# Moving the q and k transposes of four batches from TensorE to the transfer queue, with PV in quarters and in pairs

## The chip, the cores and the metric

One core of one Trainium2 chip runs the kernel. The metric is the device time of one execution in microseconds (us). Most comparisons use several rounds, in which the kernel and the kernel before ran in turn on the same chip. The start and length of each profiled execution are read from its trace.

In the profile PE is TensorE (matmul), DVE is VectorE, ACT is ScalarE, POOL is GpSimd, SP is SyncE, whose queue carries most transfers. "L754" is line 754 of that kernel's file. Lines shift between the kernels, so tile names are the safer label: b1p, op, osb, uT, qraw.

## The reference, cut to what matters

Eight batches of sparse attention (a window of 32 to each side, and eight global positions), whose result is the input of a token and channel MLP:

```python
batch, n_heads, seq, head_dim = (8, 8, 576, 64)
d_model, d_tok, d_ch = 512, 256, 1536
...
mask = (np.abs(pos[:, None] - pos[None, :]) <= 32) | is_global[:, None] | is_global[None, :]
attn = softmax(np.where(mask, scale * q @ k.T, -1e9))          # condensed
x = (attn @ v) as (batch, seq, heads * head_dim)               # condensed
h = np.maximum(xt @ w_tok1, 0.0) @ w_tok2                      # token MLP, over seq
u = x + h.transpose(0, 2, 1)
h2 = np.maximum(u @ w_ch1, 0.0) @ w_ch2                        # channel MLP
return (u + h2).astype(np.float32)
```

## The kernel before

The channel MLP of batch b is the dense part of a period: `M4` (first product, 12 groups of four matmuls into PSUM tile b1p, each evicted by ScalarE with the ReLU), then `M5` (second product, PSUM tile op, added to u by VectorE into an output buffer osb and stored). `first_half(b)` and `second_half(b)` weave attention of later batches between the dense groups. In their lists a `D` stands for one dense group; everything else is put between. The order of these lists is the order of instructions on every engine.

```python
def T(b, p):                                  # q and k of head pair p: 8 transposes on TensorE
    pT = (psm if b in (0, 2) else pss)([P, 2, 512], F16, name=f"pT_{b}_{p}")
    for ti, n in enumerate((qn, kn)):
        for i in range(4):
            nc.tensor.transpose(
                out=pT[:, ti, P * i : P * i + P], in_=n[b % 2][:, i, 2 * p : 2 * p + 2, :], identity=ident
            )
...
def TEq(b, p, eng=nc.vector.tensor_copy):     # VectorE empties PSUM, with a permutation of the columns
    eng(
        out=qTs[b % 2][:, p, 0:4, NG:QS].rearrange("p t (x i) -> p t x i", i=4),
        in_=st[b]["pT", p][:, 0].rearrange("p (i t x) -> p t x i", i=4, t=4),
    )
...
def M3(b, part):                              # u is transposed by the transfer queue for M4
    ...
            nc.sync.dma_start_transpose(out=s["uT"][:, :, P * tau : P * tau + P], in_=s["u16"][:, tau, :])
...
def M4(b, j):
    ps = psm([P, 512], name=f"b1p_{b}_{j}")   # psm: two buffers, shared with op
    for cc in range(4):
        nc.tensor.matmul(...)
    nc.scalar.activation(out=s["b1"][:, j, :], in_=ps, func=AF.Relu)
...
def M5(b, tau, part):
    ...                                       # op in psm; part 1 ends with:
        osb = ob.tile([P, DM], F32, tag="osb", name=f"osb_{b}_{tau}")
        nc.vector.tensor_add(out=osb, in0=s["u16"][:, tau], in1=ps)
        nc.sync.dma_start(out=out[b, P * tau : P * tau + P, :], in_=osb)
...
# in first_half(b), n = b + 1, m = b + 2; c(k) are two of ScalarE's casts of q and k of batch m
u = [D, D, pv(0), D, pv(1), *c(0), D, pv(2), *c(1), D, pv(3), lambda: [M1(n, ch) for ch in range(3)], *c(2), D]
u += [pv(4), *([lambda: TR(m)] if m < B else []), *tt(0), *c(3), D, lambda: M1(n, 3), D, lambda: M1(n, 4), *c(4)]
...
u += [lambda: (load_rest(m + 1), load_qk(m + 1, slice(0, H)))]        # only if m + 1 < B
u += [*tt(1), D, D, lambda: (M2(n, 0), M3(n, 0)), D, lambda: (M2(n, 1), M3(n, 1)), *tt(2), D]
```

The softmax here doesn't subtract the row's maximum and nothing guards it: scores larger than these inputs give would overflow.

Of the kernel before, what the change touches and what calls it, by code (L numbers as in the profile page):

```python
# [15 lines left out]
P = 128  # L16
NT = 5
NG = 8
# [26 lines left out]
def kernel(  # L45
# [342 lines left out]
    def casts(b):  # L388
        return [lambda ti=ti, p=p: cast_qk(b, ti, p, nc.scalar.copy) for p in (None, 0, 1, 2, 3) for ti in range(2)]
# [4 lines left out]
        )  # L394

    def T(b, p):
        pT = (psm if b in (0, 2) else pss)([P, 2, 512], F16, name=f"pT_{b}_{p}")
        for ti, n in enumerate((qn, kn)):
            for i in range(4):
                nc.tensor.transpose(  # L400
                    out=pT[:, ti, P * i : P * i + P], in_=n[b % 2][:, i, 2 * p : 2 * p + 2, :], identity=ident
                )
        st[b]["pT", p] = pT
# [13 lines left out]
    def TE(b, p):  # L417
        TEq(b, p)
        TEk(b, p)

    def TR(b):
        pr = (psm if b in (0, 2) else pss)([P, 2, 4, NP * 16], name=f"pr_{b}")
        sel = ident.rearrange("p (n r x) -> p r n x", n=NP, r=2)
        for ti, n in enumerate((qr, kr)):
            for i in range(4):
                for par in range(2):
                    nc.tensor.matmul(
                        pr[64 * par : 64 * par + 64, ti, i, :], lhsT=n[b % 2][:, i, :], rhs=sel[:, par], start=True, stop=True
                    )
        st[b]["pr"] = pr  # L430
        if b > 0:
            TRE(b)
# [214 lines left out]
    def PV(b, tau):  # L647
        s = st[b]

        sh = 64 if tau == NT - 1 and b % 2 == 1 else 0  # L650
        tiles = ((2 * tau, 0), (2 * tau + 1, 64)) if tau < NT - 1 else ((2 * tau, sh),)
        ps = (pss if b != 2 and tau % 2 else psv)([P, 2, 512], name=f"pv_{b}_{tau}")

        def glob(hf):
            for t, r0 in tiles:
                nc.tensor.matmul(  # L656
                    ps[r0 : r0 + 64, hf, 0 : NP * VW], lhsT=s["lf"][:, HQ * t : HQ * t + HQ],
                    rhs=s["rf"][:, 2 * hf : 2 * hf + 2], start=True, stop=False,
                )

        def local(hf, hh):
            h = NP * hf + hh
            for t, r0 in tiles:
                lo = QS * tau + (NG + HQ if t % 2 else NG)
                nc.tensor.matmul(  # L665
                    ps[r0 : r0 + 64, hf, VW * hh : VW * hh + VW], lhsT=e_all[:, h, lo : lo + HQ],
                    rhs=(vod if t % 2 else vsh)[b % 2][:, tau, h, :],
                    start=False, stop=hh == NP - 1,
                )

        for hf in range(2):
            glob(hf)
            for hh in range(NP):
                local(hf, hh)
        r = slice(0, P) if tau < NT - 1 else slice(sh, sh + 64)
        pq = ps[:, :, 0 : NP * VW].rearrange("p f (h x) -> p f h x", h=NP)
        rr = tiny.tile([P, 2, NP], F32, tag="rr", name=f"rr_{b}_{tau}")
        nc.vector.reciprocal(out=rr[r], in_=pq[r, :, :, D])  # L678
        nc.vector.tensor_tensor(  # L679
            out=x16s[b % 2][r, tau, :].rearrange("p (f h x) -> p f h x", f=2, h=NP), in0=pq[r, :, :, 0:D],  # L680
            in1=rr[r].unsqueeze(3).to_broadcast([P if tau < NT - 1 else 64, 2, NP, D]), op=ALU.mult,
        )
# [112 lines left out]
    def sparse2():  # L795
        b, n = 2, 3
        cs = casts(n)

        def cast(k):
            return [(0.0, c) for c in cs[2 * k : 2 * k + 2]]  # L800

        u = [(0.0, lambda: (load_rest(n), load_qk(n, slice(0, H))))]
        u += [(1.0, s2(b, 1)), (0.0, lambda: SM(b, 1)), (1.0, lambda: t(b, 3)), (1.5, s2(b, 2)), (0.0, lambda: SM(b, 2)), (0.0, lambda: v_odd(b))]
        u += [(0.3, lambda: GK(b)), (0.3, lambda: S_(b, 3, 0)), (1.8, lambda: S_(b, 3, 1)), (0.0, lambda: SM(b, 3))]
        u += [(2.5, lambda: OG(b))]
        u += [(2.0, lambda: PV(b, 0)), (2.0, lambda: PV(b, 1)), *cast(0), (2.0, lambda: PV(b, 2)), *cast(1)]
        u += [(0.0, lambda: PV(b, 3)), (1.0, lambda: [M1(b, ch) for ch in range(3)]), *cast(2)]
        u += [(2.0, lambda: PV(b, 4)), *cast(3), (3.0, lambda: [M1(b, ch) for ch in range(3, NT)]), *cast(4)]
        u += [(0.0, lambda: (load_rest(n + 1), load_qk(n + 1, slice(0, H))))]
        u += [(0.0, lambda: load_v16(n))]  # L810
        u += [(1.3, lambda: (M2(b, 0), M3(b, 0))), (1.0, lambda: (M2(b, 1), M3(b, 1)))]
        u += [(2.0, lambda: (M2(b, 2), M3(b, 2) if b % 2 else None))]
        u += [(1.0, lambda: (globals_(n), TR(n)))]
        u += [(1.2, lambda p=p: t(n, p)) for p in range(NP)]
        for p in range(NP):
            u += [(0.3, lambda p=p: S_(n, p, 0)), (2.2, lambda p=p: S_(n, p, 1)), (0.0, lambda p=p: SM(n, p))]
            if p == 2:
                u += [(0.5, lambda: GK(n)), (0.0, lambda: v_odd(n))]
        u += [(0.5, lambda: OG(n))]
        return u  # L820

    def play(steps, d):
# [27 lines left out]
        return u  # L850

    def first_half(b):
        n, m = b + 1, b + 2
        D = None
        cs = casts(m) if m < B else []

        def c(k):
            return cs[2 * k : 2 * k + 2]

        def tt(p):  # L860
            return [lambda: t(m, p)] if m < B else []

        def pv(tau):
            return lambda: PV(n, tau)

        if n == B:
            return []
        u = [D, D, pv(0), D, pv(1), *c(0), D, pv(2), *c(1), D, pv(3), lambda: [M1(n, ch) for ch in range(3)], *c(2), D]
        if b == 2:
            u += [lambda: gather_t(1)]  # L870
        u += [pv(4), *([lambda: TR(m)] if m < B else []), *tt(0), *c(3), D, lambda: M1(n, 3), D, lambda: M1(n, 4), *c(4)]
        if m < B:
            u += [lambda: load_v16(m), lambda: globals_(m)]
        if m + 1 < B:
            u += [lambda: (load_rest(m + 1), load_qk(m + 1, slice(0, H)))]
        u += [*tt(1), D, D, lambda: (M2(n, 0), M3(n, 0)), D, lambda: (M2(n, 1), M3(n, 1)), *tt(2), D]
        u += [lambda: (M2(n, 2), M3(n, 2) if n % 2 else None), D]
        return u

    def second_half(b):  # L880
        m = b + 2
        D = None
        if m >= B:
            return []
        return [D, s2(m, 0), D, lambda: t(m, 3), lambda: SM(m, 0), D, s2(m, 1), D, lambda: SM(m, 1), D, s2(m, 2), D,
                lambda: SM(m, 2), lambda: GK(m), lambda: v_odd(m), s2(m, 3), D, lambda: SM(m, 3), D, lambda: OG(m)]

    def dense(b):
# [187 lines left out]
```

## Time and profile before

| what | value |
|---|---|
| median of three runs | 345.25 us (345.13 to 349.51) |
| profiled execution | span 343.8 us |
| TensorE, VectorE, ScalarE, GpSimd busy | 91%, 56%, 45%, 19% |
| longest TensorE wait after 130 us | 1.7 us, on VectorE for pT |

### The profile page before, as it was taken

The page shows a single profiled execution, that of the slowest core. Times are in us where ns is not written, and L with a number is a line of the kernel's source. Part 1 is how long each engine was busy: PE and PEld are TensorE (multiplying, and loading weights), DVE is VectorE, ACT ScalarE, POOL GpSimd, SP SyncE. Part 2 cuts the span into 40 slices and gives each one's busy share as a digit, 9 for nine tenths or more (in the row PEclk, how much of TensorE's full clock was granted, in tenths as well). Part 3 has the DMA queues.
Part 4 walks back from the last instruction along what each step waited for, and adds up shares of the span by engine and source line. Part 5 has one row for each costly group of instructions (what it writes and reads, how often), then busy time and mean ns, then how long its engine had stood idle before and what let it go on. Part 6 is the DMA issues. An engine that isn't in the chain of part 4 may idle for free.

```text
span 343.8 us, 8245 instructions
## 1 busy us (share of the span) xinstructions
PE 312.5 (91%) x3505; PEld 170.5 (50%) x3505; DVE 192.5 (56%) x410; ACT 156.3 (45%) x281; POOL 64.2 (19%) x99
## 2 busy tenths in 40 slices
PE   4788987997999889799989999899989999999994
PEld 4557453544455435444446545444446545444641
DVE  7487268669645775557656474457746474231021
ACT  3461776515664246454456436444455433403600
POOL 5695588400030003000220003100000000000000
PEclk9999999999999999999999999999999999999998
DMA  6999998954796817698396816796102221042013
GB/s 201 207 143 233 267 177 246 208 65 96 227 89 162 219 63 86 45 259 141 62 88 198 140 70 96 60 257 148 43 0 32 63 75 51 2 113 85 2 61 92
DMA packets 78198, 41.85 MB, mean 122 GB/s; under 512 B 54482, under 2 KB 72274, under 8 KB 78162
## 3 DMA queue, kind: packets, MB, share of 16 engines
q1 hardware_dynamic: 39552, 28.45, 31.9%
q0 software_dynamic: 38608, 12.88, 31.0%
q8 instruction: 27, 0.44, 0.5%
q14 instruction: 9, 0.07, 0.1%
q10 hardware_dynamic: 2, 0.00, 0.0%
HBM read 36.11 MB, written 9.44 MB: 132 GB/s over the span
## 4 chain that ended last, share of the span: by engine, by line
PE 68%; DVE 12%; DMA 8%; issue 6%; POOL 3%; ACT 2%; SPq 1%; DVEq 0%; POOLq 0%; ACTq 0%
PE op L780 22%; PE b1p L754 21%; PE a1p L692 5%; DMA lk<-in_k_dram 5%; PE hp L716 4%; PE pv L656 4%; PE b1lp L767 3%; PE s L458 3%; PE pv L665 3%; PE pT L400 3%; DMA lv<-in_v_dram 2%; DMA lqr<-in_q_dram 1%; DVE osb L784 1%; DVE vod L373 1%; DVE vod L374 1%
## 5 line engine op out<-in xcount | busy, mean ns | idle before, releaser
L757 ACT ACTIVATE b<-b1p 128x512 f16<-128x512 f32 x96 | 57.0, 599 | 88.6 <-PE b1p L754 88.1
L754 PE MATMUL b1p<-uT,wc 128*128 128x512 f16 x384 | 94.7, 380 | 0.8 <-ACT b L757 0.6
L780 PE MATMUL op<-wc,b 128*128 128x512 f16 x384 | 90.0, 380 | 0.0
L470 ACT ACTIVATE e_all<-s 128x544 f16<-128x544 f32 (+1 forms) x64 | 40.9, 686 | 40.1 <-issue 27.2
L361 POOL DMA_DIRECT2D vsh<-in_v_dram x35 | 29.7, 851 | 142.7 <-DVE rr L678 120.5
L780 PEld LDWEIGHTS <-b 128*128 128x128 f16 x384 | 35.0, 98 | 38.9
L754 PEld LDWEIGHTS <-wc 128*128 128x128 f16 x384 | 34.6, 98 | 37.8 <-issue 2.2
L784 DVE TENSOR_TENSOR osb<-u,op 128x512 f32<-128x512 f16 x32 | 22.0, 686 | 55.8 <-PE op L780 53.9
L406 DVE COPY qT<-pT 128x512 f16<-128x512 f16 x30 | 20.6, 686 | 12.9 <-PE pT L400 11.1
L721 DVE TENSOR_TENSOR u<-x,hp 128x1024 f16<-128x1024 f16 x14 | 17.0, 1221 | 17.6 <-PE hp L716 17.6
L678 DVE RECIPROCAL rr<-pv 128x8 f32<-128x8 f32 (+1 forms) x35 | 7.2, 207 | 33.6 <-PE pv L665 33.6
L481 DVE TENSOR_TENSOR e_all<-e_all,bandm 128x616 f16<-128x616 f16 x56 | 24.4, 476 | 1.0
L679 DVE TENSOR_TENSOR x<-pv,rr 128x512 f16<-128x512 f32 (+1 forms) x35 | 24.2, 691 | 1.2
L458 PE MATMUL s<-qT,kT 64*64 64x136 f16 (+2 forms) x704 | 17.7, 216 | 5.0 <-ACT e_all L470 1.6
L412 DVE COPY kT<-pT 128x512 f16<-128x512 f16 x30 | 20.4, 681 | 1.4 <-PE pT L400 0.9
L458 PEld LDWEIGHTS <-kT 64*64 64x64 f16 x704 | 11.3, 106 | 17.0 <-issue 12.6
L656 PE MATMUL pv<-rf,lf 128*64 128x264 f16 x126 | 18.9, 287 | 0.9 <-DVE kgz L355 0.7
L716 PE MATMUL hp<-a,w 128*128 128x512 f16 x72 | 18.9, 379 | 0.0
L400 PE MATMUL pT<-ident,qn 128*128 128x128 f16 x128 | 12.9, 225 | 6.6 <-DVE kT L438 6.3
L665 PE MATMUL pv<-vsh,e_all 128*64 128x66 f16 x280 | 18.5, 194 | 0.0
L665 PEld LDWEIGHTS <-e_all 128*64 128x64 f16 x504 | 18.4, 111 | 0.0
L386 ACT CAST qn<-lq 128x512 f16<-128x512 f32 x27 | 16.6, 614 | 3.3 <-DMA lq<-in_q_dram 3.3
(175 smaller groups left out, 359.5 us busy)
## 6 DMA issues: line engine op xcount, KB each, us to landing
out_dram<-osb SPq DMA_DIRECT2D x32, 256.0 KB
lq<-in_q_dram SPq DMA_DIRECT2D x5, 1024.0 KB
lk<-in_k_dram SPq DMA_DIRECT2D x5, 1024.0 KB
wc<-in_moe_w_ch_dram POOLq DMA_DIRECT2D x6, 512.0 KB
vsh<-in_v_dram POOLq DMA_DIRECT2D x21, 128.0 KB
lq<-in_q_dram POOLq DMA_DIRECT2D x2, 1024.0 KB
lk<-in_k_dram POOLq DMA_DIRECT2D x2, 1024.0 KB
vsh<-in_v_dram POOLq DMA_DIRECT2D x14, 96.0 KB
```

Source lines behind the costliest of these rows:

```text
L361: nc.gpsimd.dma_start(out=vsh[b % 2][r0:r1, c, :, 0:D], in_=v[b, :, j0 : j0 + (r1 - r0), :].rearrange("h p d -> p h d"),)
L458: nc.tensor.matmul(ps[o, par, i0 - a : i1 - a], lhsT=kT[r, HQ * j : HQ * j + HQ], rhs=qf[r, i0:i1], start=b > 0, stop=b > 0 or j in js[-2:],)
L470: nc.scalar.activation(out=e2[:, :, a:z], in_=ps[:, :, 0 : z - a], func=AF.Exp, scale=scale)
L481: nc.vector.tensor_mul(out=e2[:, par], in0=e2[:, par], in1=bm)
L656: nc.tensor.matmul(ps[r0 : r0 + 64, hf, 0 : NP * VW], lhsT=s["lf"][:, HQ * t : HQ * t + HQ], rhs=s["rf"][:, 2 * hf : 2 * hf + 2], start=Tr ...
L665: nc.tensor.matmul(ps[r0 : r0 + 64, hf, VW * hh : VW * hh + VW], lhsT=e_all[:, h, lo : lo + HQ], rhs=(vod if t % 2 else vsh)[b % 2][:, tau ...
L679: nc.vector.tensor_tensor(out=x16s[b % 2][r, tau, :].rearrange("p (f h x) -> p f h x", f=2, h=NP), in0=pq[r, :, :, 0:D], in1=rr[r].unsquee ...
L716: nc.tensor.matmul(ps[:, i, :], lhsT=w2[:, ch, P * tau - sh : P * tau - sh + P], rhs=s["a1"][:, ch, :], start=(ch == 0), stop=(ch == 1),)
L754: nc.tensor.matmul(ps, lhsT=wc1[:, cc, P * j : P * j + P], rhs=s["uT"][:, cc, :], start=(cc == 0), stop=(cc == 3))
L757: nc.scalar.activation(out=s["b1"][:, j, :], in_=ps, func=AF.Relu)
L780: nc.tensor.matmul(ps, lhsT=w, rhs=wc2[:, j, :], start=(j == 0), stop=(j == NJ - 1))
L784: nc.vector.tensor_add(out=osb, in0=s["u16"][:, tau], in1=ps)
```

## The change

Its intent: TensorE is the bound, so take work from it. For batches 4 to 7 the 32 transposes of q and k are done by the transfer queue, as those of u already are. GpSimd casts q and k to 16 bits a period earlier; ScalarE then brings the columns into order, in eight copies a batch. The PV product uses a quarter of the TensorE array for the global products, two PV visits follow each other, and the rest rows (TR) go to PV's PSUM bank. The diff, cut to its core:

```diff
+    def QT(b, ti):
+        for i in range(4):
+            nc.sync.dma_start_transpose(
+                out=(qraw, kraw)[ti][:, :, i, :], in_=(qn, kn)[ti][b % 2][:, i].rearrange("p h d -> p (h d)")
+            )
+
+    def TS(b, p):
+        nc.scalar.copy(
+            out=qTs[b % 2][:, p, 0:4, NG:QS].rearrange("p t (x i) -> p t x i", i=4),
+            in_=qraw[:, p].rearrange("p i (t x) -> p t x i", t=4),
+        )
+        nc.scalar.copy(...)                                   # the same for k
+
+    def casts_g(b): ...                                       # ten casts by GpSimd
+    def load_next(b): ...                                     # rest rows, q and k of batch b from HBM
...
-        pr = (psm if b in (0, 2) else pss)([P, 2, 4, NP * 16], name=f"pr_{b}")
+        pr = (psm if b in (0, 2) else psv if b > 2 else pss)([P, 2, 4, NP * 16], name=f"pr_{b}")
...
         def glob(hf):
+            g = slice(HQ * hf, HQ * hf + HQ)
...
-                    ps[r0 : r0 + 64, hf, 0 : NP * VW], lhsT=s["lf"][:, HQ * t : HQ * t + HQ],
-                    rhs=s["rf"][:, 2 * hf : 2 * hf + 2], start=True, stop=False,
+                    ps[r0 : r0 + 64, hf, 0 : NP * VW], lhsT=s["lf"][g, HQ * t : HQ * t + HQ],
+                    rhs=s["rf"][g, 2 * hf : 2 * hf + 2], start=True, stop=False,
...
+        glob(0)
+        glob(1)
         for hf in range(2):
-            glob(hf)
             for hh in range(NP):
                 local(hf, hh)
...  # sparse2: the stretch of batches 0 and 1, ahead of batch 2's M4; n + 1 is 4
+        u += [(0.0, lambda: (QT(n + 1, 0), QT(n + 1, 1), load_next(n + 2)))]
...  # first_half(b), n = b + 1, m = b + 2, c = b + 3
+        u = [lambda: casts_g(c)] if c < B else []
+        u += [D, D, *ts(0), pv(0), pv(1), D, *ts(1), D, pv(2), pv(3), *ts(2), D, lambda: [M1(n, ch) for ch in range(3)], *ts(3), D]
+        if c < B:
+            u += [lambda: (QT(c, 0), QT(c, 1))]
...
+        u += [(...), lambda: load_next(c + 1), D]             # behind M3, which issues the uT transposes
```

More of the change, by code (lines that the diff above doesn't have):

```diff
@@ L396, in T @@
     def T(b, p):
-        pT = (psm if b in (0, 2) else pss)([P, 2, 512], F16, name=f"pT_{b}_{p}")
+        pT = (psm if b in (0, 2) else psv if b > 2 and p % 2 else pss)([P, 2, 512], F16, name=f"pT_{b}_{p}")
         for ti, n in enumerate((qn, kn)):
@@ L419, in TE, with casts_g, load_next @@
         TEk(b, p)
+    qraw, kraw = [const.tile([P, NP, 4, P], F16, name=f"{n}raw") for n in "qk"]
+    def QT(b, ti):
[8 more added lines that the diff above has]
+        )
+        nc.scalar.copy(
+            out=kTs[b % 2][:, p, WIN : WIN + 512].rearrange("p (x i) -> p x i", i=4),
+            in_=kraw[:, p].rearrange("p i x -> p x i"),
+        )
+    def casts_g(b):
+        for ti, p in ((0, None), (1, None), *((0, p) for p in range(NP)), *((1, p) for p in range(NP))):
+            cast_qk(b, ti, p, nc.gpsimd.tensor_copy)
+    def load_next(b):
+        if b < B:
+            load_rest(b)
+            load_qk(b, slice(0, H))
     def TR(b):
-        pr = (psm if b in (0, 2) else pss)([P, 2, 4, NP * 16], name=f"pr_{b}")
+        pr = (psm if b in (0, 2) else psv if b > 2 else pss)([P, 2, 4, NP * 16], name=f"pr_{b}")
         sel = ident.rearrange("p (n r x) -> p r n x", n=NP, r=2)
@@ L816, in sparse2 @@
             u += [(0.3, lambda p=p: S_(n, p, 0)), (2.2, lambda p=p: S_(n, p, 1)), (0.0, lambda p=p: SM(n, p))]
+            if p == 1:
+                u += [(0.0, lambda: casts_g(n + 1))]
             if p == 2:
@@ L852, in first_half, with ts @@
     def first_half(b):
-        n, m = b + 1, b + 2
+        n, m, c = b + 1, b + 2, b + 3
         D = None
-        cs = casts(m) if m < B else []
-        def c(k):
-            return cs[2 * k : 2 * k + 2]
-        def tt(p):
-            return [lambda: t(m, p)] if m < B else []
+        def ts(p):
+            return [lambda: TS(m, p)] if m < B else []
         def pv(tau):
@@ L867, in first_half @@
             return []
-        u = [D, D, pv(0), D, pv(1), *c(0), D, pv(2), *c(1), D, pv(3), lambda: [M1(n, ch) for ch in range(3)], *c(2), D]
+        u = [lambda: casts_g(c)] if c < B else []
+        u += [D, D, *ts(0), pv(0), pv(1), D, *ts(1), D, pv(2), pv(3), *ts(2), D, lambda: [M1(n, ch) for ch in range(3)], *ts(3), D]
+        if c < B:
+            u += [lambda: (QT(c, 0), QT(c, 1))]
         if b == 2:
             u += [lambda: gather_t(1)]
-        u += [pv(4), *([lambda: TR(m)] if m < B else []), *tt(0), *c(3), D, lambda: M1(n, 3), D, lambda: M1(n, 4), *c(4)]
+        u += [pv(4), D, lambda: M1(n, 3), D, *([lambda: TR(m)] if m < B else []), lambda: M1(n, 4)]
         if m < B:
             u += [lambda: load_v16(m), lambda: globals_(m)]
-        if m + 1 < B:
-            u += [lambda: (load_rest(m + 1), load_qk(m + 1, slice(0, H)))]
-        u += [*tt(1), D, D, lambda: (M2(n, 0), M3(n, 0)), D, lambda: (M2(n, 1), M3(n, 1)), *tt(2), D]
-        u += [lambda: (M2(n, 2), M3(n, 2) if n % 2 else None), D]
+        u += [D, D, lambda: (M2(n, 0), M3(n, 0)), D, lambda: (M2(n, 1), M3(n, 1)), D]
+        u += [lambda: (M2(n, 2), M3(n, 2) if n % 2 else None), lambda: load_next(c + 1), D]
         return u
@@ L884, in second_half @@
             return []
-        return [D, s2(m, 0), D, lambda: t(m, 3), lambda: SM(m, 0), D, s2(m, 1), D, lambda: SM(m, 1), D, s2(m, 2), D,
+        return [D, s2(m, 0), D, lambda: SM(m, 0), D, s2(m, 1), D, lambda: SM(m, 1), D, s2(m, 2), D,
                 lambda: SM(m, 2), lambda: GK(m), lambda: v_odd(m), s2(m, 3), D, lambda: SM(m, 3), D, lambda: OG(m)]
```

## The prediction

> **What bounds the kernel now.** I read the busy shares first, then the chain of waits, then the waits of TensorE, then the timeline of the transfer queue.
>
> ```profile
> PE 312.5 (91%) x3505; PEld 170.5 (50%) x3505; DVE 192.5 (56%) x410; ACT 156.3 (45%) x281; POOL 64.2 (19%) x99
> PE 68%; DVE 12%; DMA 8%; issue 6%; POOL 3%; ACT 2%; SPq 1%; DVEq 0%; POOLq 0%; ACTq 0%
> ```
>
> The first line has TensorE busy 91% of 343.8 us; the second says that it also makes 68% of the chain that ended last. So a microsecond of TensorE work or waiting that is removed in the middle of the kernel is worth about a microsecond, if nothing refills it. The kernel runs in periods, one for each batch of the channel MLP: 12 groups of b1p matmuls (M4), then op groups (M5), with attention of later batches woven in. M4 of batches 2, 3, 4, 5, 6 and 7 begins near 129, 166, 207, 243, 284 and 313 us. The change touches the periods of batches 1 to 6. A piece of the chain in period 2:
>
> ```profile
> 135.86 0.13 PE pv L665 x8
> 135.99 1.40 PE a1p L692 x6
> 137.39 0.86 PE b1p L754 x4
> ...
> 140.00 0.69 DVE x L679
> 140.69 0.03 issue
> 140.72 0.42 DVE qT L438
> 141.15 0.34 DVE kT L438
> 141.49 0.14 issue
> 141.62 0.61 PE pT L400 x8
> ```
>
> Columns: start, duration, what. The eight transposes of q and k of one head pair (pT) wait until VectorE has emptied the PSUM bank of the rest rows (L438). The list of waits gives the price over the kernel:
>
> ```profile
> PE pT L400 <- DVE kT L438: 6.3, 4, 1.7
> ```
>
> 6.3 us in four waits, one in each of periods 2 to 5. Other TensorE waits after 130 us are under 0.7 us each.
>
> Last, the queue of SyncE, and one end of period that shows who holds PSUM:
>
> ```profile
> 128.24 1.20 SPq L789 DMA_DIRECT2D out_dram<-osb  x2
> 149.14 6.29 SPq L733 DMA_TRANSPOSE uT<-u  x4
> ...
> 262.34 5.94 SPq L733 DMA_TRANSPOSE uT<-u  x4
> ```
>
> ```profile
> 165.98 0.61 DVE osb L784
> 166.59 0.04 issue
> 166.63 1.02 PE b1p L754 x4
> ```
>
> Four transfer transposes hold the queue for 5.94 us in an otherwise quiet stretch; single ones there start 1.31 us apart. The second fence shows that the second M4 group of a period waits for VectorE's osb addition: the op accumulator and b1p share two PSUM buffers.
>
> **What the Trainium skill says.** (1) "DMA: Bandwidth & Descriptors", section "Queues, rings and completion order": on each engine descriptors of a queue are consumed in ring order. The trace agrees: transposes issued at 149.14 us, behind two 1 MB loads issued at 146.47 and 147.41, moved their first 256-byte packets at 153.93, 4.8 us after issue; in period 5, with no load ahead, 1.2 us after (262.34 to 263.52). (2) "Advanced Engine Details and Errata", section "X-Bar Transpose (TRN2)": transpose DMAs are as fast as regular ones. The packets of one 128 KB transpose take 0.78 us, but the issue interval of 1.31 us is what limits a row of them here. (3) "TensorEngine Tiling (Array Packing)", "Key Properties": changing the tiling mode drains TensorE. The trace agrees: an M4 group next to a PV visit takes 0.97 us (period 4), elsewhere 0.86. (4) "TensorE: Matmul & The Clock Gate", Part 1: about 3.4 us of idleness can halve the clock until some 3.4 us of work. After the start this trace has no such idle stretch, so it neither shows nor denies it.
>
> **The change, part by part.**
>
> *Transposes leave TensorE.* Batches 4 to 7 lose 4 x 8 transposes each. A set of 8 without a wait takes 0.45 us in the chain (at 144.82, 149.58, 154.58), so 1.8 us a period, 7.2 us in four periods. The 6.3 us of waits for L438 go too: the rest rows now go to the PV bank, two M4 groups after it was used. Sum: 13.5 us, all on TensorE's path.
>
> *PV in quarters.* One PV visit is 0.60 us in the chain: 0.23 + 0.13 + 0.11 + 0.13. The two global products (0.23 with some 0.1 of drain, and 0.11) become one round of four quarters, about 0.12 saved. But quarters (64x64) followed by 128x64 products is one more mode change, about 0.11. A pair then has 5 changes instead of 4: saves 2 x 0.12, costs 0.1, so 0.14; two pairs 0.3 us. The last PV gains nothing, and the rest rows, before run beside it, get a visit of their own, 0.2 us. Net 0.1 us a period with rest rows, 0.3 without.
>
> *ScalarE and VectorE.* ScalarE loses 10 casts a batch (8 at 0.61, 2 at 0.40: 5.7 us) and gets 8 copies at about 0.59 (an estimate from its PSUM copies, 587 ns): 4.7 us. VectorE loses 8 copies at 0.685, 5.5 us. Neither bounds; perhaps 0.2 us a period where VectorE ends it.
>
> *GpSimd.* 10 casts a batch, 0.62 us for the large ones: about 5.8 us in a period of which it is busy 4.2 of 37. Off the path, if its input is there.
>
> *SyncE.* Eight more transposes a batch: 8 x 1.31 = 10.5 us of queue, and 11.3 us from first issue to last landing (7 x 1.31, then 1.31 + 0.78). In periods 3 to 5 there is room. In the transition there is not, and here I expect the price:
>
> 1. Transposes for batch 4 stand in the queue behind the last output store of batch 1, issued 128.24 for 1.20 us. So they start near 129.5; q has landed at 135.5, k at 140.8. ScalarE meets its copies for batch 4 after evicting two M4 groups, near 131.5, and runs in order: the evictions behind wait. TensorE does two more M4 groups and four PVs, until about 134.6, then has no PSUM for M4 group 4. It goes on after k (140.8), one copy (0.6) and one eviction (0.6): 142.0. **Wait: about 7.4 us.** ScalarE is then late, and the rest of the first half is slower by about another 0.3 us. Period 2 has lost 7.7 and gained 1.7 (wait) + 1.8 + some 0.7 for shortened PV and VectorE waits: it would end 3.5 us late, M4 of batch 3 group 1 near 170.
>
> 2. The load of batch 5 is queued behind these transposes: issued to 142.3, 2 MB took 8.0 us from first packet to last (224.75 to 232.77), so q near 146, k 149.8. GpSimd casts q until 148.5, k until 152.3. The transposes of batch 5 hold the queue from 148.6 to 159.1, uT and uTl of batch 3 (5 x 1.31) until 165.7: just in time for M4. Then the load of batch 6 is issued until 168.0, and only behind it come the output stores of batch 2. In ring order they land after its 8 us, near 176. VectorE's fourth osb needs one of three buffers, so it waits until 176, and M4 group 1 of batch 3 with it (the second fence above). **Wait: 176.7 - 170 = 6.7 us.**
>
> 3. In period 3 the stores are again behind a load (batch 7), but there a fifth op group of 2.7 us hides most of the delay; in period 4 no load follows.
>
> Sum: M4 group 1 of batch 3 is 10.1 us late (176.7 against 166.63). Periods 3, 4, 5 and 6 give back 3.4 + 3.7 + 3.4 + 0.3 = 10.8. That leaves -0.7, so 344.5 us. Period 1 may gain 1 us (alternating PSUM banks for batch 3's transposes; its waits of 0.44 and 0.78 at 116 to 118 us). Two idle stretches of 6 to 7 us may cost 1 to 2 us in clock. Together about **345 us**.
>
> **Rivals.** *A: all is hidden.* If the transposes of batch 4 start some 10 us earlier or land faster, and the stores are not held up, the gain is 13.5 + 1 + 1: about 330 us. For it: GpSimd, VectorE and the queue have the average time, and periods 3 to 5 should work. Against: a store of batch 1 stands in front in the order of issue, and the 1.31 us interval is measured. *B: only one of the two waits is real*, probably the first; the second needs the stores to land behind the load and the osb addition to hold up M4. Then some 338 us. *C: contention.* If v's 128-byte packets, the transposes and loads slow each other, or GpSimd casts slow VectorE, the chain cast, transposes, uT, stores is late in each of periods 3 to 5 too, 2 to 3 us each: some 352 us. Against it: before, DMA share in periods 2 to 4 is 0.65 to 0.73, and 8 transposes add 8 x 0.78 = 6.2 us of 37 at most, 0.17.
>
> **Range and chances.** The gain of 13.5 is firm to 1.5 us; each of the two waits is uncertain by 3 and not quite independent; the clock by 2. That gives about +-7: 337 to 352. Faster by over 2% means under 338.3: rival A or B, 0.23. Slower means over 352.2: rival C, 0.13. Within: 0.64.
>
> **What would show it.** Right: pT L400 has 128 fewer instructions and its wait for L438 is gone; in the stretch 130 to 145 us ScalarE idles on transfers into qraw and kraw, and TensorE has a gap of 6 to 8 us before a b1p group; near 170 to 178 us VectorE's osb waits for an out_dram transfer, with a second gap before b1p. Periods 3 to 5, measured between M4 starts, are 3 to 4 us shorter than before (40.3, 36.9 and 40.3). PV pairs take about 1.06 us instead of 1.20. Wrong: no gap over 2 us after 130 us (rival A); gaps in period 4 or 5 (rival C); a mode change that costs nothing, so that PV gains 0.12 each. The prediction fails most easily on the start of batch 4's transposes, because everything in periods 2 and 3 hangs on that one time.

## More of the kernel before

A table by period is the most useful view for this change. It shows the periods of batches 2 to 6 in the profile of the kernel before; the columns are stretch, length, then busy us (and instructions) of PE, PEld, DVE, ACT and POOL, then the granted TensorE clock (1.00 is full), the busy share of the DMA engines and GB/s.

```profile
128.80:165.50 36.70, 34.26 (x377) 17.51 (x376) 22.73 (x49) 18.17 (x33) 4.21 (x5) 1.00 0.76 129
165.50:206.80 41.30, 39.62 (x440) 21.24 (x436) 23.92 (x48) 19.96 (x36) 4.20 (x5) 1.00 0.64 117
206.80:242.80 36.00, 34.23 (x376) 17.37 (x375) 21.62 (x43) 18.17 (x33) 4.20 (x5) 1.00 0.71 131
242.80:284.00 41.20, 39.51 (x435) 21.15 (x435) 23.85 (x48) 19.96 (x36) 0.00 (x0) 1.00 0.18 46
284.00:312.70 28.70, 28.70 (x208) 13.77 (x207) 10.39 (x17) 7.98 (x13) 0.00 (x0) 1.00 0.24 61
```

In every period TensorE works for all but 0 to 2.4 us of the length, at full clock. VectorE and ScalarE are about half busy. Half busy is not the same as free: both empty PSUM for TensorE, and what counts for that is when they are free.

The runs of this kernel on the chips that were used lie between 344.8 and 350.2 us, so differences near one per cent need several rounds.

## The result, and the profile after

The changed kernel is correct and takes **363.43 us** (median of four runs, 361.95 to 364.73). Its ratio to the kernel before is 1.049, with a 95% interval of 1.040 to 1.058: slower, outside the predicted range. Executions over 1.5% slower than the fastest of the same kernel are left out of the means. Ratios here and below compare the fast runs of both kernels in the same rounds, so they are not quite the ratio of the medians quoted. The words that go with them (faster, same, slower, unclear) take a difference of 2% as the bar.

Three lines of the page of the changed kernel: span, busy shares, and the granted clock in tenths over forty slices.

```profile
span 362.2 us, 8046 instructions
PE 316.3 (87%) x3377; PEld 166.5 (46%) x3377; DVE 175.4 (48%) x378; ACT 167.5 (46%) x273; POOL 85.1 (23%) x139
PEclk9995999999999997699859999899999999999999
```

TensorE has 128 instructions fewer (3505 to 3377), as intended, and yet is busy for 3.8 us longer, because its clock was halved in four stretches (27.7 to 38.0, 140.4 to 150.6, 177.9 to 191.6 and 229.1 to 232.5 us): each 5 to 8 in the last line is part of one.

The list of TensorE's waits, then of VectorE's and ScalarE's (columns: who waits and for which tile, for whom; us in total, times, longest):

```profile
PE b1p L783 <- DVE osb L813: 12.8, 2, 10.1
PE b1p L783 <- ACT b L786: 12.7, 6, 9.4
...
DVE osb L813 <- DMA out_dram<-osb: 16.1, 3, 9.9
...
ACT kT L434 <- DMA kraw<-kn: 5.7, 1, 5.7
ACT qT L430 <- DMA qraw<-qn: 4.7, 1, 4.7
```

Two waits before a b1p group, of 10.1 and 9.4 us, stand where none over 0.6 us stood. The wait of pT for L438 (6.3 us) is gone. Read from the bottom: ScalarE waited once for q and once for k; VectorE waited for output stores to leave their buffers; TensorE waited for each of them. The timeline of period 2 and the start of period 3 puts that in order (start, duration; in brackets the wait before it and what ended it):

```profile
137.46 1.06 ACT L430 COPY qT<-qraw 128x512 f16<-128x512 f16 x1 [4.72 <-DMA qraw<-qn]
144.24 1.05 ACT L434 COPY kT<-kraw 128x512 f16<-128x512 f16 x1 [5.71 <-DMA kraw<-kn]
145.19 0.59 ACT L786 ACTIVATE b<-b1p 128x512 f16<-128x512 f32 x1
145.83 1.86 PE L783 MATMUL b1p<-uT,wc 128*128 128x512 f16 x4 [9.44 <-ACT b L786]
...
185.39 0.69 DVE L813 TENSOR_TENSOR osb<-u,op 128x512 f32<-128x512 f16 x1 [9.91 <-DMA out_dram<-osb]
186.13 1.87 PE L783 MATMUL b1p<-uT,wc 128*128 128x512 f16 x4 [10.07 <-DVE osb L813]
```

The first wait is a chain of four links: k lands, ScalarE copies it, then evicts an M4 group, then TensorE goes on. The second is: a store lands, VectorE adds, TensorE goes on. The last line also tells of the clock: four matmuls took 1.87 us where 1.02 us was the time of such a group before (166.63). And the queue of SyncE shows why the transfers came so late:

```profile
129.68 1.20 SPq L818 DMA_DIRECT2D out_dram<-osb  x2
130.97 5.17 SPq L425 DMA_TRANSPOSE qraw<-qn  x4
136.67 6.26 SPq L425 DMA_TRANSPOSE kraw<-kn  x4
144.41 0.46 SPq L116 DMA_DIRECT2D lq<-in_q_dram  x1
154.90 5.15 SPq L425 DMA_TRANSPOSE qraw<-qn  x4
...
171.36 1.21 SPq L765 DMA_TRANSPOSE uTl<-ul  x1
173.97 0.46 SPq L116 DMA_DIRECT2D lq<-in_q_dram  x1
174.48 0.57 SPq L116 DMA_DIRECT2D lk<-in_k_dram  x1
175.16 11.28 SPq L814 DMA_DIRECT2D out_dram<-osb  x4
```

Everything waits for what stands in front of it: the transposes for batch 4 follow the last store of batch 1 (129.68), the load of batch 5 follows those transposes (144.41), the transposes of batch 5 need that load (154.90), and the four stores of batch 2 come behind the load of batch 6 (175.16). The page of this kernel gives ScalarE's copies in section 5 (count, busy us, mean ns):

```profile
L434 ACT COPY kT<-kraw 128x512 f16<-128x512 f16 x16 | 17.1, 1071 | 5.7 <-DMA kraw<-kn 5.7
L430 ACT COPY qT<-qraw 128x512 f16<-128x512 f16 x16 | 17.1, 1067 | 4.7 <-DMA qraw<-qn 4.7
```

1.07 us each, where the prediction had 0.59. That came from this line of the kernel before, a copy with the same permutation that reads PSUM:

```profile
L406 ACT COPY qT<-pT 128x512 f16<-128x512 f16 x2 | 1.2, 587 | 2.2 <-issue 1.3 <-PE pT L400 0.9
```

Finally the table by period, in the same columns as before:

```profile
130.20:175.00 44.80, 34.58 (x349) 15.92 (x344) 18.10 (x41) 21.17 (x31) 9.50 (x15) 0.89 0.81 137
175.00:229.00 54.00, 40.14 (x407) 19.69 (x403) 18.83 (x40) 22.83 (x34) 14.07 (x24) 0.87 0.74 160
229.00:263.90 34.90, 33.81 (x343) 15.41 (x343) 16.91 (x36) 20.93 (x31) 9.26 (x12) 0.95 0.92 122
263.90:302.70 38.80, 37.67 (x406) 19.01 (x404) 18.91 (x40) 22.73 (x34) 0.00 (x0) 1.00 0.16 49
302.70:331.10 28.40, 28.40 (x207) 13.25 (x206) 10.21 (x17) 7.97 (x13) 0.00 (x0) 1.00 0.24 61
```

Against the table of before, period 2 is 8.1 us longer and period 3 12.7 us longer. Period 4 is 1.1 us and period 5 is 2.4 us shorter: in the one period with full clock and no long wait the change does give something back, but less than the 3.4 us predicted. The whole of the loss lies in two periods.

### The profile page after: what moved, and what is told of

Its sections match the earlier page's. It is cut to its first block, busy times and chain, and to the rows that moved or that the text cites. A ratio compares the mean times of both kernels' runs of the same rounds, so it can differ in the third digit from the quotient of the medians.

```text
span 362.2 us, 8046 instructions
## 1 busy us (share of the span) xinstructions
PE 316.3 (87%) x3377; PEld 166.5 (46%) x3377; DVE 175.4 (48%) x378; ACT 167.5 (46%) x273; POOL 85.1 (23%) x139
## 4 chain that ended last, share of the span: by engine, by line
PE 63%; DVE 12%; ACT 10%; DMA 7%; SPq 3%; issue 3%; DVEq 0%; ACTq 0%
PE op L809 21%; PE b1p L783 17%; DMA out_dram<-osb 6%; PE hp L745 4%; PE a1p L721 3%; ACT kT L434 3%; PE b1lp L796 3%; ACT qT L430 3%; SPq L425 3%; PE s L485 3%; ACT b L786 2%; PE pv L693 2%; DVE kT L412 2%; DVE osb L813 1%; DVE qT L406 1%
## 5 line engine op out<-in xcount | busy, mean ns | idle before, releaser
L783 PE MATMUL b1p<-uT,wc 128*128 128x512 f16 x384 | 98.2, 393 | 25.6 <-DVE osb L813 12.8
L783 PEld LDWEIGHTS <-wc 128*128 128x128 f16 x384 | 36.2, 100 | 69.0 <-issue 32.6
L383 POOL CAST qr<-lqr 128x256 f16<-128x256 f32 x5 | 2.0, 399 | 100.4 <-DMA lqr<-in_q_dram 100.4
L434 ACT COPY kT<-kraw 128x512 f16<-128x512 f16 x16 | 17.1, 1071 | 5.7 <-DMA kraw<-kn 5.7
L430 ACT COPY qT<-qraw 128x512 f16<-128x512 f16 x16 | 17.1, 1067 | 4.7 <-DMA qraw<-qn 4.7
L386 POOL CAST qn<-lq 128x512 f16<-128x512 f32 x18 | 10.4, 614 | 23.9 <-PE pT L400 10.3
L693 PE MATMUL pv<-vsh,e_all 128*64 128x66 f16 x280 | 15.9, 200 | 0.0
L721 PE MATMUL a1p<-x,w 128*128 128x512 f16 x56 | 15.5, 406 | 0.0
L693 PEld LDWEIGHTS <-e_all 128*64 128x64 f16 x504 | 12.0, 113 | 4.6 <-issue 0.5
```

The costliest lines, as they stand in the source:

```text
L430: nc.scalar.copy(out=qTs[b % 2][:, p, 0:4, NG:QS].rearrange("p t (x i) -> p t x i", i=4), in_=qraw[:, p].rearrange("p i (t x) -> p t x i", ...
L434: nc.scalar.copy(out=kTs[b % 2][:, p, WIN : WIN + 512].rearrange("p (x i) -> p x i", i=4), in_=kraw[:, p].rearrange("p i x -> p x i"),)
L693: nc.tensor.matmul(ps[r0 : r0 + 64, hf, VW * hh : VW * hh + VW], lhsT=e_all[:, h, lo : lo + HQ], rhs=(vod if t % 2 else vsh)[b % 2][:, tau ...
L721: nc.tensor.matmul(ps[tt], lhsT=w, rhs=x16s[b % 2][:, ch, :], start=(ch == 0), stop=(ch == NT - 1))
L783: nc.tensor.matmul(ps, lhsT=wc1[:, cc, P * j : P * j + P], rhs=s["uT"][:, cc, :], start=(cc == 0), stop=(cc == 3))
```

## The experiments

Twelve kernels ran, all with the right result. The first two undo the cause of one long wait each, the third both; then come the cheap part of the gain, the clock, the copies, PV, and four steps towards a better version.

### 1. Transposes of batch 4 earlier (e1_early)

The theory was that the first wait is a matter of place in the queue. GpSimd's casts for batch 4 and the transposes move forward, the latter between two output stores of batch 1:

```diff
                 nc.sync.dma_start(out=out[b, P * tau : P * tau + P, :], in_=osb)
+                if b == 1 and tau == 1:
+                    QT(4, 0)
+                    QT(4, 1)
...
-        u += [(0.0, lambda: (QT(n + 1, 0), QT(n + 1, 1), load_next(n + 2)))]
+        u += [(0.0, lambda: load_next(n + 2))]
```

> The changed kernel, with one thing moved: the transposes of batch 4 are issued between the second and third output store of batch 1, near 119 us, rather than behind the last store at 131 us. Theory (the first wait is the queue of SyncE): ScalarE no longer idles 4.7 and 5.7 us on qraw and kraw, the 9.44 us gap of TensorE before a b1p group shrinks under 1.5 us, the half clock from 140 to 151 us goes, 10 to 12 us in all: about 352 us. The second wait stays, 9 to 11 us. Rival (the slow copies of ScalarE, 1.07 us each, are what holds M4): under 3 us change.

Measured: 354.51 us (352.32 to 357.62), ratio 1.020 (1.009 to 1.032), in words "unclear". TensorE's waits in its profile:

```profile
PE b1p L783 <- DVE osb L813: 13.6, 2, 10.8
PE b1p L783 <- ACT b L786: 2.7, 5, 1.0
```

The 9.4 us wait for ScalarE is gone, with the half clock that followed it (none from 140 to 151 us), and the kernel is some 9 us faster than the changed one by the medians. The second wait stands, at 10.8 us. So the first wait came from the place of those eight transfers in the queue (their casts had to move with them), and it can be removed without the second.

### 2. Loads ahead of the uT transposes (e2_loadup)

The theory was that the second wait is stores behind a load. The load is issued right behind the q and k transposes, ahead of uT and of the stores:

```diff
-            u += [lambda: (QT(c, 0), QT(c, 1))]
+            u += [lambda: (QT(c, 0), QT(c, 1), load_next(c + 1))]
...
-        u += [lambda: (M2(n, 2), M3(n, 2) if n % 2 else None), lambda: load_next(c + 1), D]
+        u += [lambda: (M2(n, 2), M3(n, 2) if n % 2 else None), D]
```

> The changed kernel, with one thing moved: in each period the load of q and k is issued right behind the transposes of q and k and ahead of uT, so that the output stores no longer stand behind it. Theory (the second wait is the store behind the load in ring order): VectorE's osb wait for out_dram falls from 9.9 to about 2 us, the gap of 10.07 us to about 2 to 3, the 2.75 us gap at 229 and both half clock stretches behind them go: 12 to 15 us, about 350 us. The first wait stays 9.4. Rival (the stores are late because the whole chain of transposes is late, whatever stands ahead): osb still waits 7 us or more, under 4 us change.

Measured: 355.64 us (351.96 to 357.6), ratio 1.020 (1.010 to 1.030), unclear. The execution that was profiled fell in the slow state, so only its order of events is used. The wait of b1p for osb is down from 10.1 to 0.5 us; in its place b1p waits 6.9 us for uT, whose transposes are now behind the load:

```profile
PE b1p L783 <- DMA uT<-u: 6.9, 1, 6.9
```

The store order was the cause of the second wait, but with a load of 2 MB ahead of uT most of it comes back in another place. By the medians the kernel is some 8 us faster than the changed one, less than the 12 to 15 us expected.

### 3. Both (e3_both)

> Both moves. Theory: the two waits are the loss; together about 338 us, at least 5 us below the kernel before, with no half clock after 45 us. Rival (something else costs, such as ScalarE's copies or the transfers): 345 us or more.

Both edits together give 347.60 us (347.08 to 350.57), ratio 1.004 (0.995 to 1.012): the same as the kernel before. All of the 18 us loss but 2 is undone by two changes of order. What is left, in its list of waits and in its timeline:

```profile
PE b1p L783 <- DMA uT<-u: 6.9, 1, 6.9
...
155.77 0.46 SPq L116 DMA_DIRECT2D lq<-in_q_dram  x1
157.93 9.68 SPq L762 DMA_TRANSPOSE uT<-u  x4
169.64 1.86 PE L783 MATMUL b1p<-uT,wc 128*128 128x512 f16 x4 [6.91 <-DMA uT<-u]
```

The load is issued at 155.77, the four uT transposes behind it need 9.68 us of queue instead of about 6, and TensorE waits 6.91 us for them. The wait has moved from the stores to uT: whatever stands behind a load pays for it. Three waits of b1p for ScalarE (2.7 us in all) and two of og, the matmuls for the rows of the global positions, for VectorE (3.1 us) are left as well, and the kernel is some 10 us slower than the 338 us expected.

### 4. The cheap part of the gain, without any transfer (e4_banks)

6.3 us of the expected gain was the wait of pT for the rest rows' bank. Here only that is taken, from the kernel before: rest rows in the PV bank, two M4 groups later, and the first pair's transposes with them.

```diff
-        pr = (psm if b in (0, 2) else pss)([P, 2, 4, NP * 16], name=f"pr_{b}")
+        pr = (psm if b in (0, 2) else psv if b > 2 else pss)([P, 2, 4, NP * 16], name=f"pr_{b}")
...
-        u += [pv(4), *([lambda: TR(m)] if m < B else []), *tt(0), *c(3), D, lambda: M1(n, 3), D, lambda: M1(n, 4), *c(4)]
+        u += [pv(4), *c(3), D, lambda: M1(n, 3), D, *([lambda: TR(m)] if m < B else []), *tt(0), lambda: M1(n, 4), *c(4)]
```

> The kernel before, with the rest rows put into the PV bank and visited two M4 groups after the last PV, TensorE transposes kept. Theory: the wait of pT for L438 (6.3 us in four periods) goes without any transfer transpose, and the visit of its own costs 0.2 us a period: about 339.5 us. Rival (the wait turns into another, on the PSUM bank of pT or on VectorE): within 2 us of before.

Measured: 345.84 us (344.92 to 346.7), ratio 0.996 (0.988 to 1.003), the same. A line of its timeline tells why:

```profile
221.88 0.38 PE L400 MATMUL pT<-ident,qn 128*128 128x128 f16 x4 [1.11 <-ACT a L700]
```

The wait for VectorE became a wait of 1.1 us for ScalarE, which empties the token MLP's tile `a` in the same pool. Four such waits take 4.5 us of the 6.3 back. Taking away what ended a wait isn't worth the wait if the next thing in line is nearly as late.

### 5. How much of the loss is clock (e5_warm)

A rival explanation of the size was the halved clock after each wait. Dummy matmuls fill the two waits of the changed kernel, 150 in the first and 160 in the second:

```diff
+    def W3(pool, n):
+        w = pool([P, 2, 512], name="warm3")
+        for _ in range(n):
+            nc.tensor.matmul(w[:, 0, 0:P], lhsT=ident, rhs=ident, start=True, stop=True)
...
+   W3(pss, 160) behind the first D if b == 3; W3(psv, 150) behind pv(3) if b == 2
```

> The changed kernel with dummy matmuls (results unused) put into TensorE's two long waits: 150 of 128 columns ahead of M4 group 4 of batch 2, 160 ahead of M4 group 1 of batch 3; the waits themselves stay. Theory (idle waits cost a second time through the clock): the half clock stretches at 140 to 151 and 178 to 192 us vanish, 4 to 5 us faster than the changed kernel, about 359 us, though work was added. Rival (the half clock has another cause, or TensorE is then not the limit): 363 us or more.

Measured: 362.60 us (360.32 to 362.79), ratio 1.042 (1.037 to 1.048), about 1 us below the changed kernel's median. The half clock from 140 to 151 us is gone, and that after 178 us but for 3.4 us. Yet the first op group of batch 2 starts at 160.69 us instead of 161.45, that of batch 3 at 209.19 instead of 209.74. So in period 2 the 4.8 us of half clock after the wait cost only 0.8 us: TensorE isn't what limits that stretch. ScalarE is behind with copies of 1.07 us each in its queue, and M4 goes at ScalarE's pace: at full clock four M4 groups in a row (146.03 to 153.31 us) still start 2.4 us apart, and one eviction and two copies take ScalarE 2.4 us (150.00 to 152.40 us in the changed kernel). The slow clock is mostly an effect beside the cause.

### 6. Copies that read in order (e6_inorder)

If ScalarE's 1.07 us came from reading every 128th element, reading in order and writing every fourth would cure it:

```diff
-            out=kTs[b % 2][:, p, WIN : WIN + 512].rearrange("p (x i) -> p x i", i=4),
-            in_=kraw[:, p].rearrange("p i x -> p x i"),
+            out=kTs[b % 2][:, p, WIN : WIN + 512].rearrange("p (x i) -> p i x", i=4),
+            in_=kraw[:, p],
```

(and q alike.)

> The changed kernel, with ScalarE's 32 copies reading qraw and kraw in order and writing every fourth element (before: reading with a step of 256 bytes, writing in order). Theory (the strided read is why a copy takes 1.07 us): copies near 0.6 us, the gaps of 0.75 to 0.96 us before b1p in periods 3 to 5 go, the transposes of batch 5 start some 3.5 us earlier and the second wait shrinks by that: 6 to 9 us, about 356 us. Rival (SBUF source or output pattern is what costs): still 1.0 us or more, no change of time.

Measured: 366.16 us (363.65 to 368.08), ratio 1.055 (1.048 to 1.061).

```profile
L434 ACT COPY kT<-kraw 128x512 f16<-128x512 f16 x16 | 22.3, 1395 | 3.1 <-DMA kraw<-kn 3.1
L430 ACT COPY qT<-qraw 128x512 f16<-128x512 f16 x16 | 21.1, 1320 | 6.6 <-DMA qraw<-qn 6.6
```

The copies became slower, 1.32 and 1.40 us. That theory fell: a strided write is dearer here than a strided read. No run has a copy on ScalarE that both reads SBUF and writes it in order, so how much of the 1.07 us is the stride and how much the source stays open.

### 7 and 8. The best order, with either kind of copy (e7_all, e9_order)

To experiment 3 is added that the load of batch 5 comes right behind the early transposes; e7 has the in-order copies, e9 the original ones.

```diff
                     QT(4, 1)
+                    load_next(5)
...
-        u += [(0.0, lambda: load_next(n + 2))]
```

> Early transposes of batch 4, then at once the load of batch 5; loads ahead of uT in every period; copies that read in order. Theory: no wait above 2 us is left, the removed transposes and the 6.3 us of waits count: about 336 us, faster than the kernel before by over 2%. Rival (uT behind the load is late, as in the run with both moves): 343 us or more, with a b1p gap on uT of 4 us or more. If copies do not get faster, also about 343.

> As the run with everything, but with the copies as the change has them (1.07 us, against 1.32 to 1.40 when they write with a stride). Theory: the slower copies cost that run the gaps of 1.3 us before b1p and held the transposes of batch 5; with 1.07 us it is 3 to 5 us faster than it: 341 to 343 us. Rival (what is left of the loss is the loads and stores in the one queue, not the copies): 345 to 346 us, as before.

Measured: e7 346.21 us (345.09 to 348.93), ratio 0.999 (0.993 to 1.005); e9 345.19 us (341.31 to 349.58, two of its runs slow), ratio 0.987 (0.981 to 0.993); both are "same" by the bar of 2%. In e7 TensorE waits ten times for ScalarE's eviction, 8.6 us in all and 1.3 us at most; in e9 three such waits after 130 us are 0.76 to 0.96 us each. Both missed their theory (336, and 341 to 343 us); the fast runs of e9 have a mean of 343.4 us, between its theory and its rival, and its profile still has waits of 2.4 us for uT and 3.6 us of og for VectorE, so how much of the rest is the copies isn't settled here. With the order right the change is worth about 1%.

### 9. PV alone (e8_pv)

The kernel before with quarters and pairs only:

```diff
-                    ps[r0 : r0 + 64, hf, 0 : NP * VW], lhsT=s["lf"][:, HQ * t : HQ * t + HQ],
+                    ps[r0 : r0 + 64, hf, 0 : NP * VW], lhsT=s["lf"][HQ * hf : HQ * hf + HQ, HQ * t : HQ * t + HQ],
...                # rhs alike; glob(0), glob(1) ahead of the locals; pv(0), pv(1) and pv(2), pv(3) side by side
```

> The kernel before with the PV part alone: quarters and pairs. As predicted: 0.3 us a period in periods 2 to 6, 1.5 us faster. After the trace of the changed kernel, where a visit takes 0.61 us against 0.60: no change within 1 us. Rival (the mode change is free): 3 us faster.

Measured: 348.38 us (344.41 to 351.72, two runs slow), ratio 1.004 (0.998 to 1.009), the same. Its timeline in period 3 shows a pair between M4 groups:

```profile
167.13 0.31 PE L656 MATMUL pv<-rf,lf 64*64 64x264 f16 x4
167.75 0.31 PE L656 MATMUL pv<-rf,lf 64*64 64x264 f16 x4
168.36 1.90 PE L755 MATMUL b1p<-uT,wc 128*128 128x512 f16 x8
```

From start to start a visit takes 0.62 and 0.61 us, against 0.60 before. The four quarters do run at once, but the first local product now starts 0.24 us after the global ones instead of 0.13. Two M4 groups and two visits take 3.06 us, against twice 1.57 before: 0.08 saved, by the pairing.

### 10. The copies shared out (e10_split)

From e9: q is copied by VectorE at the places where it used to empty pT, from two raw buffers, k by ScalarE.

```diff
-    qraw, kraw = [const.tile([P, NP, 4, P], F16, name=f"{n}raw") for n in "qk"]
+    qraw = [const.tile([P, NP, 4, P], F16, name=f"qraw{i}") for i in range(2)]
+    kraw = const.tile([P, NP, 4, P], F16, name="kraw")
...
-    def TS(b, p):
-        nc.scalar.copy(
+    def TSq(b, p):
+        nc.vector.tensor_copy(
```

> As that, but q is copied by VectorE at the places where it emptied PSUM before, from two raw buffers, and ScalarE copies k alone. Theory: ScalarE no longer holds M4 evictions (gaps of 0.96 us gone), the transposes of q need not wait for ScalarE: 337 to 340 us, faster than the kernel before by 1.5 to 2.5%. Rival: VectorE's copy from SBUF with a strided read is also near 1.07 us or more and VectorE then ends the periods (og waits for eg): 343 us or more.

Measured: 339.32 us (336.11 to 340.09), ratio 0.975 (0.970 to 0.979), faster.

```profile
L437 ACT COPY kT<-kraw 128x512 f16<-128x512 f16 x16 | 17.1, 1070 | 0.0
L431 DVE COPY qT<-qraw 128x512 f16<-128x512 f16 x16 | 10.4, 652 | 0.1
```

The copy of q takes 652 ns on VectorE, against 1067 ns on ScalarE in the changed kernel. M4's waits for ScalarE after 130 us, 0.76 to 0.96 us each in e9, are gone. The edit also gives q a second raw buffer; what that is worth by itself was not run. One long wait is left: 4.4 us for uT, behind the load.

### 11. The kernel before, with the waits nearly gone (e11_banks2)

Experiment 4 with the second pair's transposes one M4 group later, behind ScalarE's `a`:

```diff
-        u += [*tt(1), D, D, lambda: (M2(n, 0), M3(n, 0)), D, ...]
+        u += [D, *tt(1), D, lambda: (M2(n, 0), M3(n, 0)), D, ...]
```

> The kernel before with the rest rows in the PV bank as in the earlier run, and the transposes of the second pair moved behind one more M4 group. In the earlier run the wait of pT had turned from VectorE's copy of the rest rows (1.5 to 1.7 us) into ScalarE's activation of a1p (1.1 us). Theory (it is one PSUM bank, free about 1 us later): under 0.4 us of wait left a period, 4 x 1.2 less 0.2 each for the extra visit, 341 to 342 us. Rival (it turns into another wait again): 344 us or more.

Measured: 341.86 us (340.4 to 344.38), ratio 0.985 (0.981 to 0.990): "same" by the bar of 2%, but clear of no change. Four short pT waits are left of the 6.3 us:

```profile
PE pT L400 <- ACT a L700: 1.1, 4, 0.3
```

About 5 us of the 6.3 is to be had by another PSUM bank for the rest rows and by moving three entries in a list (the rest rows and two sets of transposes), with no transfer, cast or copy added.

### 12. The load behind the stores (e12_loadend)

From e10: the load is issued at the end of a period, behind the output stores, so that neither uT nor a store stands behind it.

```diff
-            u += [lambda: (QT(c, 0), QT(c, 1), load_next(c + 1))]
+            u += [lambda: (QT(c, 0), QT(c, 1))]
...
-                ..., D, lambda: SM(m, 3), D, lambda: OG(m)]
+                ..., D, lambda: SM(m, 3), D, lambda: OG(m), lambda: load_next(b + 4)]
```

> As the split copies, but the load of q and k stands behind the output stores, at the end of each period, so that neither uT nor the stores are behind it. Theory (ring order: whatever stands behind 2 MB of load lands 8 us late): the last wait of that run, 4.4 us of b1p on uT, and its half clock of 6.8 us go; the load lands some 10 us into the next period, in time for casts, and no b1p or og gap over 1.6 us is left after 130 us: 332 to 335 us, faster than before by over 2%. Rival (transposes of q and k, now later because of their casts, push uT late in turn): a b1p gap on uT of 3 us or more, 338 us or more.

Measured: **333.69 us** (330.83 to 336.0, one run slow), ratio 0.954 (0.949 to 0.959). It beats both kernels. The kernel before was at its slow end in these rounds (ten of its eleven runs lay between 347.9 and 350.0 us); against its 345.25 us of the first measurement the medians differ by 3.3%. The longest waits that are left (both of og before 130 us), and three periods, in the columns of the tables above:

```profile
PE og L569 <- DVE eg L506: 2.6, 2, 1.6
...
PE b1p L786 <- DMA uT<-u: 1.5, 1, 1.5
```

```profile
130.00:163.00 33.00, 32.22 (x350) 15.33 (x346) 20.55 (x46) 17.48 (x27) 9.93 (x15) 1.00 1.00 181
163.00:200.70 37.70, 37.45 (x406) 18.97 (x404) 21.77 (x44) 19.28 (x30) 10.62 (x15) 1.00 0.92 168
200.70:234.40 33.70, 32.12 (x343) 15.05 (x342) 19.42 (x39) 17.49 (x27) 14.28 (x20) 1.00 1.33 170
```

These three periods are 3.7, 3.6 and 2.3 us shorter than before, at full clock. In two of them the predicted yield, 3.4 to 3.7 us a period, is there once nothing gives it back.

## Why the prediction was wrong

It said 345.0 us, and the same time within 2% with a chance of 0.64; it is 363.4 us. Its list of causes was nearly right and its sizes were not. Its sum gave -0.7 us before small corrections; between the two profiled executions the end moved by +18.5 us (343.8 to 362.2). The prediction's period lengths before (40.3, 36.9 and 40.3 us) mix the first and the second M4 group; between the starts of M4 they are 41.3, 36.0 and 41.3, as in the table above. The 19.2 us between -0.7 and +18.5, by stretches; a stretch is how much later an event is in the profile after than before, less the same at the event above it:

| stretch, up to | predicted | measured | difference |
|---|---|---|---|
| M4 of batch 2 | 0 | +1.4 | 1.4 |
| where M4 group 1 of batch 3 begins to wait (first wait, less gains) | +3.4 | +8.0 | 4.6 |
| M4 group 1 of batch 3 (second wait) | +6.7 | +10.1 | 3.4 |
| M4 of batch 4 | -3.4 | +2.75 | 6.1 |
| M4 of batch 5 | -3.7 | -1.1 | 2.6 |
| M4 of batch 6 | -3.4 | -2.5 | 0.9 |
| the end | -0.3 | -0.1 | 0.2 |

**Right.** The 128 transposes and the 6.3 us of waits did leave TensorE. PV was worth almost nothing (experiment 9; the text had 0.1 to 0.3 us a period), though a pair takes 1.23 us, not the 1.06 named as a sign. Both waits came, at the places and through the links that were foretold: ScalarE's copies ahead of evictions, and stores behind the load of batch 6. Experiments 1 to 3 show each to be a matter of queue order. Of the rivals, C, "late in each of periods 3 to 5 too", is nearest in time (352); the loss came by another mechanism, two waits in periods 2 and 3. The sign that periods 3 to 5 would be 3 to 4 us shorter failed: by the tables they were 12.7 us longer, 1.1 and 2.4 us shorter.

**Step 1, the size of the first wait: 9.4 us, not 7.4.** One of the k transposes took 2.3 us to issue where 1.25 us was usual, and SyncE paused half a microsecond between q and k, so k was there at 144.2 us, not 140.8; the other 1.5 us of that come from the later start of the first transpose (130.97 us), which moved TensorE's work too. The copy behind k took 1.05 us, not 0.6.

**The estimate of ScalarE's copy: 0.59 us, measured 1.07.** This is the term that failed most widely. It was taken from copies of the same shape and permutation that read PSUM, but these read SBUF. So ScalarE did not lose 1 us of work a batch (5.7 against 4.7); it got 8.6 instead, about 3 us more. The trace had no instruction of that kind on ScalarE, and the text gave the estimate no range. It is why the first half of period 2 goes on at ScalarE's pace after the wait (experiment 5: full clock, only 0.8 us better), where "another 0.3 us" had been allowed. It is also why each later period has a TensorE wait of 0.76 to 0.96 us for ScalarE's eviction (experiment 10: with half of the copies on VectorE these are gone).

**Step 2, the size of the second wait: 10.1 us, not 6.7.** The chain of transfers ran later at each link. The load of q of batch 5, issued at 144.4, landed at 152.4, 8.0 us later, where the prediction allowed some 4, half of the 8 us of the whole load. Even in the kernel before the q of such a load needed more than that, 5.5 us (issued at 223.69). Why it and that one transpose of k were slower now was not tested; contention between the transfers, of which rival C spoke, is possible and not shown. So the transposes of batch 5 were issued at 154.9, not 148.6, and the loads and stores behind them 7 us later than thought.

**Step 3, "hides most of the delay": wrong.** Period 3 was to give back 3.4 us and lost 2.75. By its timeline, the osb addition ahead of batch 4's M4 waited 4.3 us for a store behind the next load, and TensorE 2.75 us for it; one wait for ScalarE was 0.76; and after the wait the clock was half for 5.4 us, worth an estimated 2.7 us (half of that stretch, if all of it was TensorE's work). With the estimate these make 6.2 us, against the 6.1 of the table.

**The clock: 1 to 2 us were allowed.** Besides period 3, period 4 had 3.4 us at half clock, an estimated 1.7 us by the same reckoning, which with a wait of 0.96 us for ScalarE makes the 2.6 of the table. The 1.4 us ahead of M4 of batch 2 goes with a half clock between 27.7 and 38.0 us at the start of this execution; a variant of the kernel before (experiment 9) has a shorter one, at 12.3 to 15.7 us, and runs of the kernel before had mean granted clocks down to 0.977 against 0.996 in its profile, so I don't count it to the change; this is argued and not shown. Why it comes in some executions is open. Open too is how much of the loss the clock makes by itself in period 3: experiment 5 could fill the second wait only in part. There the half clock behind that wait lasted 3.4 us instead of 5.4, and from M4 group 1 of batch 3 to its first op group 22.4 us passed instead of 23.6, which is in line with the reckoning by halves.

The weighing was wrong with the sizes. The text set the first wait and the second each uncertain by 3 us and rival C at 0.13, yet three of its terms (q's landing, the copy, the store in period 3) erred towards later, and two of them hung on one queue.

## What to carry to other kernels

A transfer queue that works in order is an engine like any other: write down its issue times for the whole stretch before moving work to it, and put first what TensorE waits for, last what has a period to spare; order alone was worth 16 to 18 us here, and the same work made the kernel slower by 5% or, ordered and shared out, faster by 3 to 5%. An instruction kind that the trace doesn't have on that engine with that source has no price yet: run it once before it carries a sum. And ask first which part of a gain needs the new mechanism: 5 us of it could be had by another PSUM bank and three moved entries in a list.

## What the Trainium skill lacked or had wrong

- No page gives the price of a strided copy on ScalarE from SBUF; what the pages say of strides in general has no figure for it. Copies of 128x512 in 16 bits took 1.07 us with a strided read and 1.32 to 1.40 us with a strided write, against 0.587 us with the same permutation read from PSUM; the strided-read copy of q took 0.652 us on VectorE.
- "Advanced Engine Details and Errata", section "X-Bar Transpose (TRN2)", calls transpose transfers as fast as regular ones. A row of them is limited by issue here: 1.31 us for each 128 KB, of which 0.78 us is movement. That makes about 100 GB/s, an estimate from these numbers, where 2 MB of plain load in 8.0 us make about 260. In experiment 3, behind a load, four took 9.7 us to issue.
- "TensorE: Matmul & The Clock Gate", Part 1, gives an idle window of about 3.4 us as the cause of a halved clock; it also tells of a kernel in which frequent short idle times were enough, without saying how short. In e7 one wait of 1.93 us (162.52 to 164.45) came ahead of a half clock from 164.88 to 171.71 us. In the changed kernel half clock lasted 3.4 to 13.7 us; behind the two long waits it went on for 4.8 and 5.4 us after work had begun again.
